# Attention steps inside a feed-forward stream: later mask products and row turns, a fourth rotating PSUM bank, one more step turned by TensorE

## The chip, the cores and the metric

The kernel runs on one core of one Trainium2 chip. The metric is the device time of one execution in microseconds (us), from the start to the end of the program on that core. Times are given as the median over several executions; a profile is one more execution, recorded by the hardware profiler, with its own time.

## What is computed

Eight batches of eight heads go through a windowed causal attention over 576 positions of 64 channels; the result is laid out as 4608 rows of 512 channels and goes through a multiplicative feed-forward network. Heads 0 to 3 look at the last 32 positions ("plain"), heads 4 to 7 at every fourth of the last 128 ("dilated").

```
scores = scale * np.matmul(q, k.transpose(0, 1, 3, 2))        # [8, 8, 576, 576]
mask_plain = (rel >= 0) & (rel < 32)
mask_dil = (rel >= 0) & (rel < 128) & (rel % 4 == 0)
attn = softmax(where(mask, scores, -1e9))
x = (attn @ v).transpose(0, 2, 1, 3).reshape(4608, 512)
a = x @ w1                    # 512 -> 1024
b = x @ w2
h = a * b @ w3                # 1024 -> 1024
out = h @ w_out               # 1024 -> 512
```

## The kernel before

**Tiling.** A batch's attention is cut into four *steps*, numbered 4b to 4b+3: the two halves of the positions for the dilated heads (u = 1; steps 4b and 4b+1), then the two halves for the plain heads (u = 0; steps 4b+2 and 4b+3). A step handles four heads and 288 positions. Its stations are:

- `scores`: 24 small matmuls into the four-bank PSUM tile `ps_a` (L313), one exponential over 128x1152 on ScalarE into the SBUF tile `et` (L343), and one product of `et` with the 0/1 mask on VectorE, in place (L344). In the kernel before, all three are emitted together.
- `values`: 12 matmuls with `et` as weights (L355) into another part of `ps_a`, then a reciprocal (L363) and a product (L366) on VectorE that leave the normalised rows in `xo`.
- `to_channels`: `xo` has to be turned so that channels lie on partitions, into `XT[u]`. Either six TensorE transposes into PSUM (L413) and a ScalarE copy (L419), or one transposing DMA on SyncE's queue (L404). The flag `by_dma` (L297) says which; before, it is true from step 8 on but for steps 10 and 11.

Queries and keys are loaded as rows (`qn`, `kn`) by GpSimd's DMA queue and turned on VectorE by stream transposes (L269, L277) into `qt` and `kt`; a batch needs 14 such *row turns*: four for each of dilated q, dilated k and plain q, and two longer ones for plain k. `qn` and `kn` have two buffers each, so the load for batch b+2 (L138) waits until the last row turn has read batch b's buffer. The stretch `prefetch(b)` emits the loads of q, k, the dilated v (`vd`) and the plain v (`vp`) in this order on GpSimd's queue.

**The feed-forward part.** w3 and w_out are first multiplied into one matrix `wf_sb` (`fuse_t`: transposes of w3 rows, L662 and L668; `fuse_m`: L676 and L684). Then, for each batch and half hf of the positions and each of eight blocks f, `ffn1` runs two *halves*, one with w1 and one with w2: four matmuls of 128x128 weights against 128x288 columns of `XT` each (L579), in the order dilated, dilated, plain, plain. The first half's sum is copied to SBUF by ScalarE (`asb`, L612), the second is multiplied with it on VectorE into `gt` (L619). `ffn2` takes a tile of 128 rows: eight matmuls over 512 columns (L646), a ScalarE copy (L653) and stores on SyncE's queue (L628).

**PSUM.** `bank()` hands out PSUM banks in rotation: three buffers called `f`. The eighth bank, `ps_x`, is used by `to_channels` and the first `fuse_t`; it joins the rotation as every fourth bank once batch 1 is done (L759 and L760). A half can only start when the reader of the bank's last contents (the copy L612 or L653, or the product L619) is done.

**Order of the work.** All is emitted in one order, written by the program, and each engine runs its instructions in that order. The feed-forward loops call `point(n)` before each half (0.57 units) and each half of an `ffn2` tile (1 unit). The attention is a list of *phases*, each with some `room`; `point` emits phases until the place in that list reaches what a straight line between `marks` asks for at this count of units. A mark says by which count a batch's steps must all be emitted: at the start of that batch's `ffn1`, less `ahead` units. `segment` builds the list for steps 8 to 31: in round i come `scores` of step i, an empty phase with two row turns, the turn of step i-2 where TensorE does it, `values` of step i-1 (with its transposing DMA, where DMA does it), and an empty phase with two more row turns. `second_batch` lists steps 4 to 7 with a fixed count of units for each. Batch 0 is emitted ahead of all this by `first_batch`.

Four banks of rotation and its order are decided in these lines:

```python
def bank():
    if "x" in late:
        late["x"] += 1
        if late["x"] % 4 == 0:
            return ps_x.bitcast(F32)
    return banks.tile([P, TB], F32, tag="f", name="f")
```

Of the kernel before, what the change touches and what calls it, by code (L numbers as in the profile page):

```python
# [12 lines left out]
BF16 = mybir.dt.bfloat16  # L13
# [3 lines left out]
ACT = mybir.ActivationFunctionType  # L17
# [6 lines left out]
HALF = 288  # L24
# [29 lines left out]
def kernel(  # L54
# [11 lines left out]
    nc = tc.nc  # L66
# [6 lines left out]
    KFF = d_ff // P  # L73
    NT = n_tok // TB
    scale = 1.0 / float(np.sqrt(D))
# [42 lines left out]
    ps_x = psum.tile([P, 2 * TB], BF16, name="ps_x")  # L118
    pool = four_banks()
    ps_s = [pool.tile([P, 2, TB], F32, name=f"ps_s{i}") for i in range(2)]  # L120
    late = {}
# [7 lines that stand above are left out]
# [163 lines left out]
    class Step:  # L292
        def __init__(self, n, b, u, hf):
            self.b, self.u, self.hf = b, u, hf
            self.et = ets[n % NET]

            self.by_dma = b > 2 or (b == 2 and u == 1)  # L297
            self.xo = {}

        def score_matmuls(self, heads, bank_of, start):  # L300
# [36 lines left out]
        def scores(self):  # L337

            ps_a = late["a"]
            self.score_matmuls(range(4), lambda h: ps_a[:, h], True)  # L340
            ev = self.probs(0, 4)
            mk = (mask_di if self.u else mask_pl[:, self.hf]).rearrange("p m x -> p (m x)")
            nc.scalar.activation(out=ev, in_=ps_a[:, :, 0:HALF], func=ACT.Exp, scale=scale)  # L343
            nc.vector.tensor_tensor(  # L344
                out=ev, in0=ev, in1=mk.unsqueeze(1).to_broadcast([P, 4, HALF]), op=AL.mult
            )
# [51 lines left out]
                        self.value_matmul(2 * hp + hl, m, ov[:, j // 3, j % 3, :])  # L398
            self.normalize(ov, self.xo.rearrange("p h j d -> p (h j) d"), 4, 3)()

        def to_channels(self, ps=ps_x, copy=nc.scalar.copy, hps=(0, 1)):
            dst = XT[self.u][:, 2 * self.b + self.hf]
            if self.by_dma:
                nc.sync.dma_start(  # L404
                    out=dst.rearrange("p h (m t) -> p (h m) t", m=3),
                    in_=self.xo[0:96].rearrange("p h (m e) d -> p (h m) (e d)", m=3),
                    transpose=True,
                )
                return
            xv = ps[:, 0 : 2 * HALF].rearrange("p (h x) -> p h x", h=2)  # L410
            for hp in hps:
                for m in range(3):
                    nc.tensor.transpose(  # L413
                        out=xv[:, hp, 96 * m : 96 * m + 96],
                        in_=self.xo[0:96, hp, 2 * m : 2 * m + 2, :],
                        identity=ident[0:96, 0:96],
                    )
            h = slice(hps[0], hps[-1] + 1)
            copy(out=dst[:, h], in_=xv[:, h])  # L419
# [3 lines left out]
    steps = [  # L423
        Step(4 * b + 2 * (1 - u) + hf, b, u, hf)
        for b in range(B)
        for u in (1, 0)
        for hf in range(2)
    ]
# [10 lines left out]
    def later(f, *args, after=1.0):  # L439

        phases.append([lambda: f(*args)])
        room.append(after)
# [5 lines left out]
    def first_batch():  # L448


        d0, d1, p0, p1 = steps[0:4]
        transpose_qk(0, 1, 0)
        transpose_qk(0, 1, 1)
        d0.scores_of_pair(0)
        d0.scores_of_pair(1)
        transpose_qk(0, 0, 0)
        d1.scores_of_pair(0)
        d1.scores_of_pair(1)
        transpose_qk(0, 0, 1)
        warm_up(4)  # L460
        p0.scores_of_pair(0)
        p0.scores_of_pair(1)
        warm_up(2)
        d0.values_of_pair(0)
        d0.values_of_pair(1)
        p1.scores_of_pair(0)
        warm_up(1)
        d1.values_of_pair(0)
        d1.values_of_pair(1)
        p1.scores_of_pair(1)  # L470
        d0.to_channels()
        p0.values_of_pair(0)
        p1.values_of_pair(0)
        pool = four_banks()
        ps_b = [pool.tile([P, TB], F32, name=f"ps_b{i}") for i in range(4)]
        late.update(b=ps_b, n=0)
        d1.to_channels(ps_b[0].bitcast(BF16))
        warm_up(1, ps_b[3])
        p0.values_of_pair(1)
        p0.to_channels(ps_x, hps=(0,))  # L480
        p1.values_of_pair(1)
        begin(0, 0, (2, 3))
        begin(0, 1, (2, 3))
        begin(0, 0, (0,))
        begin(0, 1, (0,))
        p0.to_channels(ps_x, hps=(1,))
        x1 = bank().bitcast(BF16)
        p1.to_channels(x1, nc.vector.tensor_copy, hps=(0,))
        begin(1, 0, (2, 3))
        begin(1, 1, (2, 3))  # L490
        begin(0, 0, (1,))
        begin(0, 1, (1,))
        p1.to_channels(x1, nc.vector.tensor_copy, hps=(1,))
        begin(1, 0, (0,))
        begin(1, 1, (0,))
        ffn1(0, 0, 0)
        begin(1, 0, (1,))
        begin(1, 1, (1,))
        const_masks()
        prefetch(2)  # L500
# [3 lines left out]
    def second_batch():  # L504

        d0, d1, p0, p1 = steps[4:8]
        for at, f, *args in (
            (19, transpose_qk, 1, 1, 0),
            (20, transpose_qk, 1, 1, 1),
            (22, d0.scores),  # L510
            (24, d1.scores),
            (26, d0.values),
            (26, transpose_qk, 1, 0, 0),
            (27, transpose_qk, 1, 0, 1),
            (28, d0.to_channels),
            (28, d1.values),
            (31, p0.scores),
            (32, d1.to_channels),
            (33, p1.scores),
            (35, p0.values),  # L520
            (37, p0.to_channels),
            (37, p1.values),
            (37, prefetch, 3),
            (37, transpose_qk, 2, 1, 0),
            (38, transpose_qk, 2, 1, 1),
            (39, p1.to_channels),
            (39, transpose_qk, 2, 0, 0),
        ):
            later(f, *args)
            when.append(at)  # L530

    def segment(lo, hi):


        pieces = []

        def some():
            for f in pieces[:2]:
                behind(f)
            del pieces[:2]  # L540

        for i in range(lo, hi + 1):
            at, b = i % 4, i // 4
            more = 4 * (b + 1) < hi
            if at == 0 and i < hi:
                pieces += transposes(b, 0, 1)
                for u, which in ((1, 0), (1, 1), (0, 0)) if more else ():
                    pieces += transposes(b + 1, u, which)
            if i < hi:
                later(steps[i].scores, after=0.8)  # L550
                later(lambda: None, after=0.8)
                some()
            if i > lo + 1 and not steps[i - 2].by_dma:
                later(steps[i - 2].to_channels, after=0.4)
                done_at[i - 2] = len(phases)
            if i > lo:
                later(steps[i - 1].values, after=0.8)
                if steps[i - 1].by_dma:
                    behind(steps[i - 1].to_channels)
                done_at[i - 1] = len(phases)  # L560
                if i < hi:
                    later(lambda: None, after=0.8)
                    some()
            if at == 2:
                behind(prefetch, b + 2)

# [89 lines left out]
    w3T = {}  # L656

    def fuse_t(ft):
        xv = bank().bitcast(BF16) if ft else ps_x
        xv = xv.rearrange("p (g x) -> p g x", g=KFF)  # L660
        for g in range(KFF):
            nc.tensor.transpose(  # L662
                out=xv[:, g, :],
                in_=w3n[ft // 2][:, ft % 2, g * P : (g + 1) * P],
                identity=ident,
            )
        w3T[ft] = wk_pool.tile([P, KFF, P], BF16, tag="w3T", bufs=3, name="w3T")
        nc.scalar.copy(out=w3T[ft], in_=xv)  # L668
# [44 lines left out]
    n0 = len(when)  # L713
    marks = [(40, n0)]
    for b in range(2, B):
        ahead = (0, 3, 6)[min(b - 2, 2)]
        marks.append((40 + 27.25 * (b - 1) - ahead, done_at[4 * b + 3]))
    place = np.concatenate([[0.0], np.cumsum(room)])
    xs, ys = [m[0] for m in marks], [place[m[1]] for m in marks]
# [1 line left out]
    def point(n):  # L721
        state[0] += n
        want = int(np.searchsorted(place, np.interp(state[0], xs, ys) - 1e-6))
        while state[1] < want and (state[1] >= n0 or state[0] >= when[state[1]]):
            for f in phases[state[1]]:
                f()
            state[1] += 1

    for f in range(1, KFF + 2):
        if f < KFF:  # L730
            ffn1(0, 0, f)
        if f == KFF:
            fuse_t(0)
        if f >= 2:
            ffn1(0, 1, f - 2)
# [14 lines left out]
    for b in range(1, B):  # L750
        for hf in range(2):
            for f in range(KFF):
                ffn1(b, hf, f, point)
                if due and f in (1, 3, 5):
                    ffn2(due.pop(0), point)
            while P * (done + 1) <= b * S + (hf + 1) * HALF:
                due.append(done)
                done += 1
        if b == 1:  # L759
            late["x"] = 0  # L760
    for t in due:
        ffn2(t, point)
    assert state[1] == len(phases)
# [30 lines left out]
```

## Time and profile before

| | us |
|---|---|
| median of 13 executions (lowest to highest) | 256.64 (255.66 to 257.82) |
| the profiled execution's own time | 257.65 |
| its span on the core, first to last instruction | 255.9 |
| TensorE (PE) matmuls busy in the span | 248.8 |
| VectorE (DVE) busy | 161.4 |
| ScalarE (ACT) busy | 119.4 |
| batch 1's feed-forward part begins, at TensorE | 64.1 |
| batch 2's begins (about) | 88.5 |

In the profile's rows a line such as L579 is the line of the kernel, followed by the engine, the operation, what it writes and reads, and how often. PE is TensorE's matmuls, PEld its weight loads, POOL is GpSimd, SP is SyncE. In a timeline row the first number is the start in us from the span's start, the second the duration; equal neighbours are merged, and "x8" says of how many instructions a row is made. Matmuls are pipelined, and the end of each is modelled, so the duration of one matmul (286 ns for 288 columns) is longer than the time from one start to the next. In a weight-load row, square brackets give the idle time ahead of it.

### The profile page before, as it was taken

The page shows a single profiled execution, that of the slowest core. Times are in us where ns is not written, and L with a number is a line of the kernel's source. Part 1 is how long each engine was busy: PE and PEld are TensorE (multiplying, and loading weights), DVE is VectorE, ACT ScalarE, POOL GpSimd, SP SyncE. Part 2 cuts the span into 40 slices and gives each one's busy share as a digit, 9 for nine tenths or more (in the row PEclk, how much of TensorE's full clock was granted, in tenths as well). Part 3 has the DMA queues.
Part 4 walks back from the last instruction along what each step waited for, and adds up shares of the span by engine and source line. Part 5 has one row for each costly group of instructions (what it writes and reads, how often), then busy time and mean ns, then how long its engine had stood idle before and what let it go on. Part 6 is the DMA issues. An engine that isn't in the chain of part 4 may idle for free.

```text
span 255.9 us, 6683 instructions
## 1 busy us (share of the span) xinstructions
PE 248.8 (97%) x2700; PEld 165.1 (65%) x2700; DVE 161.4 (63%) x379; ACT 119.4 (47%) x220; POOL 59.9 (23%) x87
## 2 busy tenths in 40 slices
PE   7899999999999999998999999999999999999995
PEld 2477764645665766665676766676767666777663
DVE  6676436867878766566685775577767543645550
ACT  2454356564644654544445444444444445333332
POOL 8984333737205201501061106000000000000000
DMA  6999999999999993999479957931313222312113
GB/s 102 166 188 200 206 212 200 190 201 204 252 191 153 170 214 89 144 180 160 92 105 163 186 102 111 158 88 35 96 26 94 57 64 67 105 29 79 40 44 123
DMA packets 66562, 33.81 MB, mean 132 GB/s; under 512 B 51556, under 2 KB 56932, under 8 KB 66532
## 3 DMA queue, kind: packets, MB, share of 16 engines
q0 software_dynamic: 47232, 20.70, 66.9%
q1 hardware_dynamic: 19300, 12.69, 21.9%
q8 instruction: 21, 0.34, 0.6%
q14 instruction: 9, 0.07, 0.1%
HBM read 41.39 MB, written 9.44 MB: 199 GB/s over the span
## 4 chain that ended last, share of the span: by engine, by line
PE 72%; DMA 19%; DVE 2%; POOL 2%; ACT 2%; issue 1%; POOLq 0%
PE f L579 30%; PE f L646 18%; PE ps_x L579 8%; DMA w3n<-in_moe_w_dram 6%; DMA XT<-xo 6%; PE ps_x L646 5%; DMA w_sb<-in_moe_w_dram 4%; PE ps_a L355 4%; PE f L676 3%; PE ps_a L313 3%; DMA kn<-in_k_dram 2%; POOL w_sb L177 2%; ACT et L343 2%; PE f L662 1%; PE ps_x L413 1%
## 5 line engine op out<-in xcount | busy, mean ns | idle before, releaser
L579 PEld LDWEIGHTS <-w_sb 128*128 128x128 bf16 x1024 | 97.2, 98 | 32.1 <-issue 3.3
L579 PE MATMUL f<-XT,w_sb 128*128 128x288 bf16 x704 | 100.8, 286 | 1.4 <-DMA XT<-xo 0.8
L619 DVE TENSOR_TENSOR gt<-f,asb 128x288 bf16<-128x288 f32 x91 | 45.2, 504 | 18.7 <-PE f L579 18.6
L646 PE MATMUL f<-wf_sb,gt 128*128 128x512 bf16 (+1 forms) x240 | 55.9, 372 | 0.0
L612 ACT CAST asb<-f 128x288 bf16<-128x288 f32 x85 | 34.0, 400 | 34.7 <-PE f L579 32.3
L646 PEld LDWEIGHTS <-gt 128*128 128x128 bf16 x296 | 27.7, 98 | 25.5
L343 ACT ACTIVATE et<-ps_a 128x1152 bf16<-128x1152 f32 x28 | 31.7, 1132 | 10.3 <-PE ps_a L313 10.3
L653 ACT COPY osb<-f 128x512 f32<-128x512 f32 (+1 forms) x30 | 17.1, 571 | 39.7 <-PE f L646 39.4
L166 POOL DMA_DIRECT2D vd<-in_v_dram x32 | 21.2, 670 | 54.3 <-PE ps_a L355 47.4
L579 PE MATMUL ps_x<-XT,w_sb 128*128 128x288 bf16 x192 | 31.4, 286 | 0.0
L366 DVE TENSOR_TENSOR xo<-ps_a,rcp 96x768 bf16<-96x768 f32 x28 | 26.7, 954 | 1.0
L344 DVE TENSOR_TENSOR et<-et,mask_pl 128x1152 bf16<-128x1152 bf16 x14 | 10.6, 759 | 19.2 <-ACT et L343 19.2
L277 DVE STREAM_TRANSPOSE qt<-qn 128x160 uint32<-128x160 uint32 (+1 forms) x64 | 21.2, 423 | 2.0 <-DMA qn<-in_q_dram 1.9
L344 DVE TENSOR_TENSOR et<-et,mask_di 128x1152 bf16<-128x1152 bf16 x14 | 10.6, 759 | 18.1 <-ACT et L343 18.1
L313 PEld LDWEIGHTS <-kt 32*128 32x128 bf16 x768 | 10.6, 92 | 11.9 <-issue 8.6
L355 PEld LDWEIGHTS <-et 128*128 128x128 bf16 x384 | 16.0, 98 | 3.4 <-ACT et L333 0.2
L579 PE MATMUL ps_b<-XT,w_sb 128*128 128x288 bf16 x128 | 16.5, 286 | 0.0
L612 ACT CAST asb<-ps_x 128x288 bf16<-128x288 f32 x27 | 10.8, 399 | 11.2 <-PE ps_x L579 11.2
L676 PE MATMUL f<-wo_sb,w3T 128*128 128x512 bf16 x64 | 16.0, 379 | 0.0
L646 PE MATMUL ps_x<-wf_sb,gt 128*128 128x512 bf16 x56 | 13.2, 379 | 0.0
L619 DVE TENSOR_TENSOR gt<-ps_x,asb 128x288 bf16<-128x288 f32 x21 | 10.2, 485 | 4.3 <-PE ps_x L579 4.3
L313 PE MATMUL ps_a<-qt,kt 32*128 32x96 bf16 x672 | 12.3, 202 | 0.2 <-DVE kt L277 0.2
(71 smaller groups left out, 178.1 us busy)
## 6 DMA issues: line engine op xcount, KB each, us to landing
out_dram<-osb SPq DMA_DIRECT2D x28, 144.0 KB
qn<-in_q_dram POOLq DMA_DIRECT2D x6, 576.0 KB, 10.0
kn<-in_k_dram POOLq DMA_DIRECT2D x6, 576.0 KB, 10.5
w_sb<-in_moe_w_dram POOLq DMA_DIRECT2D x8, 256.0 KB, 8.1
w3n<-in_moe_w_dram POOLq DMA_DIRECT2D x4, 512.0 KB, 14.2
vp<-in_v_dram POOLq DMA_DIRECT2D x5, 384.0 KB, 8.0
out_dram<-osb SPq DMA_DIRECT2D x10, 128.0 KB
qn<-in_q_dram POOLq DMA_DIRECT2D x4, 288.0 KB, 6.9
```

Of the source, the lines that this page charges most:

```text
L166: nc.gpsimd.dma_start(out=vds[b % 2][p0 : p0 + n, 4 * m : 4 * m + 4, 16 : 16 + 2 * D], in_=bass.AP(tensor=x.tensor, offset=x.offset + (4 * ...
L277: nc.vector.transpose(out=bass.AP(tensor=o.tensor, offset=o.offset + at, ap=[o.ap[0], [1, n], [9, 16], [step, 2]],), in_=t[:, k : k + 4 * ...
L313: nc.tensor.matmul(out=bank_of(h)[:, c0 : c0 + 96], lhsT=kt[prt, 96 * m : 96 * m + P, c], rhs=rhs, start=(start and c == 0), stop=(c == 1 ...
L343: nc.scalar.activation(out=ev, in_=ps_a[:, :, 0:HALF], func=ACT.Exp, scale=scale)
L344: nc.vector.tensor_tensor(out=ev, in0=ev, in1=mk.unsqueeze(1).to_broadcast([P, 4, HALF]), op=AL.mult)
L355: nc.tensor.matmul(out=out, lhsT=self.et[:, c0 : c0 + P], rhs=rhs, start=True, stop=True)
L366: nc.vector.tensor_tensor(out=xo[0:96].rearrange("p (n k) d -> p n k d", n=n), in0=ov[0:96, :, :, x0 : x0 + D], in1=rcp[0:96].unsqueeze(3) ...
L579: nc.tensor.matmul(out=ps[:, 0:HALF], lhsT=w_sb[:, c, f * P : (f + 1) * P], rhs=x, start=(c == 2), stop=(c == 1),)
L612: nc.scalar.copy(out=a_sb, in_=ps[:, 0:HALF])
L619: nc.vector.tensor_tensor(out=g, in0=pb, in1=a_sb, op=AL.mult)
L646: nc.tensor.matmul(out=y, lhsT=gt[:, f, g0 : g0 + P], rhs=wf_sb[:, f, c0 : c0 + n], start=(f == 0), stop=(f == KFF - 1),)
L676: nc.tensor.matmul(out=wf_ps[ft], lhsT=w3T[ft][:, g, :], rhs=wo_sb[:, g, :], start=(g == 0), stop=(g == KFF - 1),)
```

## The change

The mask product becomes a method of its own, `mask`, emitted one phase after the exponential, in the phase that was empty (and in `second_batch` by counts of its own). The row turns that prepare the next batch are spread differently over the four rounds of a batch: two behind the first round's scores, none behind its mask or values; then none and two; two and two; three and three. They stand behind the scores and no longer behind an empty phase after them. `ps_x` is in the rotation from the first `fuse_t` on, and `to_channels` and every `fuse_t` take their bank from the rotation. Step 9 (batch 2, dilated, second half) is turned by TensorE. The mark of batch 3 is set four units ahead, not three.

```diff
-            self.by_dma = b > 2 or (b == 2 and u == 1)
+            self.by_dma = b > 2 or (b, u, hf) == (2, 1, 0)
...
             ev = self.probs(0, 4)
+            nc.scalar.activation(out=ev, in_=ps_a[:, :, 0:HALF], func=ACT.Exp, scale=scale)
+
+        def mask(self):
+            ev = self.probs(0, 4)
             mk = (mask_di if self.u else mask_pl[:, self.hf]).rearrange("p m x -> p (m x)")
-            nc.scalar.activation(out=ev, in_=ps_a[:, :, 0:HALF], func=ACT.Exp, scale=scale)
             nc.vector.tensor_tensor(
...
-        def to_channels(self, ps=ps_x, copy=nc.scalar.copy, hps=(0, 1)):
+        def to_channels(self, ps=None, copy=nc.scalar.copy, hps=(0, 1)):
...
+            if ps is None:
+                ps = bank().bitcast(BF16)
...
             (22, d0.scores),
+            (23, d0.mask),
             (24, d1.scores),
+            (25, d1.mask),
...
             (32, d1.to_channels),
+            (32, p0.mask),
             (33, p1.scores),
+            (34, p1.mask),
...
-        def some():
-            for f in pieces[:2]:
+        def some(n):
+            for f in pieces[:n]:
                 behind(f)
-            del pieces[:2]
+            del pieces[:n]
...
+            n = ((2, 0), (0, 2), (2, 2), (3, 3))[at]
             if i < hi:
                 later(steps[i].scores, after=0.8)
-                later(lambda: None, after=0.8)
-                some()
+                some(n[0])
+                later(steps[i].mask, after=0.8)
...
                 if i < hi:
                     later(lambda: None, after=0.8)
-                    some()
+            if i < hi:
+                some(n[1])
...
     def fuse_t(ft):
-        xv = bank().bitcast(BF16) if ft else ps_x
-        xv = xv.rearrange("p (g x) -> p g x", g=KFF)
+        xv = bank().bitcast(BF16).rearrange("p (g x) -> p g x", g=KFF)
...
-        ahead = (0, 3, 6)[min(b - 2, 2)]
+        ahead = (0, 4, 6)[min(b - 2, 2)]
...
+    late["x"] = 0
     for f in range(1, KFF + 2):
...
-        if b == 1:
-            late["x"] = 0
```

More of the change, by code (lines that the diff above doesn't have):

```diff
@@ L470, in first_batch @@
         p1.scores_of_pair(1)
-        d0.to_channels()
+        d0.to_channels(ps_x)
         p0.values_of_pair(0)
```

## The prediction, made before the changed kernel was run

> **What bounds the kernel now.** I read the page's first part, then the waits, then the timeline of TensorE against its own pitch, then the chain.
>
> ```profile
> PE 248.8 (97%) x2700; PEld 165.1 (65%) x2700; DVE 161.4 (63%) x379; ACT 119.4 (47%) x220; POOL 59.9 (23%) x87
> ...
> L619 DVE TENSOR_TENSOR gt<-f,asb 128x288 bf16<-128x288 f32 x91 | 45.2, 504 | 18.7 <-PE f L579 18.6
> ...
> L343 ACT ACTIVATE et<-ps_a 128x1152 bf16<-128x1152 f32 x28 | 31.7, 1132 | 10.3 <-PE ps_a L313 10.3
> ...
> L344 DVE TENSOR_TENSOR et<-et,mask_pl 128x1152 bf16<-128x1152 bf16 x14 | 10.6, 759 | 19.2 <-ACT et L343 19.2
> ```
>
> TensorE is busy for 248.8 of 255.9 us, so at most 7.1 us of visible idle time can be won, part of it before the first operands arrive. The mask product (0.76 us) idles VectorE for 37.3 us in all (the waits: 27 times, 1.4 us each), because it stands in VectorE's queue right behind an exponential of 1.13 us. That is idle time of an engine at 63%; it costs only where TensorE waits for the `gt` products queued behind it.
>
> Whether it does can't be read from "busy", because ends of matmuls are modelled. The starts tell it. A row without a stall is the first below: 12 matmuls in 1.63 us, of which 0.16 is the last one's modelled tail, so 0.1225 us a matmul and 0.49 us a half of `ffn1`. The next rows are batch 1, with three banks:
>
> ```profile
> 129.27 1.63 PE L579 MATMUL f<-XT,w_sb 128*128 128x288 bf16 x12
> ```
> ```profile
> 64.10 2.34 PE L579 MATMUL f<-XT,w_sb 128*128 128x288 bf16 x16
> ...
> 72.69 3.12 PE L579 MATMUL f<-XT,w_sb 128*128 128x288 bf16 x20
> ...
> 73.98 0.76 DVE L344 TENSOR_TENSOR et<-et,mask_pl 128x1152 bf16<-128x1152 bf16 x1 [1.25 <-ACT et L343]
> 74.39 0.46 PEld L579 LDWEIGHTS <-w_sb 128*128 128x128 bf16 x4 [0.24 <-issue]
> 74.65 0.45 DVE L619 TENSOR_TENSOR gt<-f,asb 128x288 bf16<-128x288 f32 x1
> ...
> 75.16 0.34 PEld L579 LDWEIGHTS <-w_sb 128*128 128x128 bf16 x3 [0.31 <-issue]
> ```
>
> Twenty matmuls should take 20 x 0.1225 + 0.16 = 2.61 us; the row has 3.12, so 0.51 us was lost. TensorE's next weights come at 75.16, just after the product of 74.65 ended at 75.10 and freed its bank; that product stood behind the mask, the mask behind the exponential. The same subtraction over 64 to 91 us gives 0.22 (64.10), 0.39 (66.75: 8 matmuls end their pitch at 67.73, the next start is 68.12), 0.16 (68.12), 0.16 (70.11), 0.51 (72.69), 0.22 (83.72, a copy behind an exponential on ScalarE) and 0.11 (87.51): **1.77 us for want of a bank.** At 92.77 the turn of step 11 waits 0.23 us for `ps_x`, which a half has just used. From there on, with four banks and the same masks, no such row is left; two stalls remain, and the chain names them:
>
> ```profile
> 108.50 1.28 PE f L579 x11
> 109.78 8.18 DMA XT<-xo
> 118.00 0.90 PE f L579 x6
> ...
> 136.94 7.26 DMA XT<-xo
> 144.25 0.41 PE f L579 x2
> ```
>
> These are the transposing DMAs of steps 14 and 18, the plain first halves of batches 3 and 4. `ffn1` of the batch needs them at its third matmul. By the pitch TensorE was due at 117.03 and at 144.0, so the stalls are 0.97 and 0.27 us. Their packets are late because loads are in the same DMA engines: in the trace the transfer of step 24, with no load about, is through 2.1 us after its issue, that of step 14 7.7 us after. Recoverable in all: 1.77 + 0.23 + 0.97 + 0.27 = **3.24 us**.
>
> **The change, part by part.**
>
> *Fourth bank.* With three banks TensorE has two other halves, 0.98 us, before it needs a bank again; with four, 1.47 us, or 1.23 where a turn (six transposes, 0.26) takes a slot. The longest stall of the 1.77 is 0.39 us and the 0.51 is a 0.22 and a 0.29, all below the 0.49 gained. Turns and `fuse_t` now share the rotation. Their copies (L419 0.64, L668 1.01 us, ScalarE) end long before their bank returns: after `fuse_t` come a `fuse_m` of 1.73 us and more. I count that as nothing; it hides behind those matmuls, and without that cover a turn would hold its bank 0.64 - 0.40 = 0.24 us longer than a half.
>
> *Mask one phase later.* A phase is 1.7 units, some 1.46 us of TensorE work (an `ffn2` half is one unit and four matmuls of 0.217 us). The exponential ends about 0.4 + 0.1 + 1.13 = 1.65 us after the scores begin; the mask, emitted 1.46 us later and behind the `gt` products in between, finds it done. Nobody new waits: `values` of step i-1 come after the mask of step i, so each mask has a whole step (6.5 us and more) until its matmuls. In the second batch the shortest distance is the mask of step 7, at 34, to its values at 37: over 2.5 us of matmuls against 0.76. Cost nothing, if VectorE keeps up, which is the next point.
>
> *Row turns.* Their number stays. I worked the emission order out from the pacing arithmetic. Between the scores of step 8 and tile 4 of `ffn2`, batch 1's dense stretch, VectorE now has two long k turns (1.40), masks 8 to 10 (2.28), ten `gt` (5.04), four q turns (1.69) and two normalisations (2 x (0.22 + 0.95) = 2.34): 12.75 us. TensorE has 20 halves (9.8), three scores (0.37 + 0.22 of entry and exit each: 1.8) and two values (0.7): 12.3 us. Before, two more turns stood here (0.85) and some 4 us of waiting for exponentials. So VectorE falls behind by about 0.45 us plus what it brings along, against up to 1 us of bank slack. I keep **0.4 us** of the 3.24 as not won; the ends are 0 (slack holds) and 0.9 (half of the bank stalls stay). The turns also release loads on GpSimd's queue. Before, step 14's DMA (issue 109.78) had the load of `qn` for batch 6 beside it, issued at 108.38 just after the last q turn of batch 4. Now these three turns come behind two halves and their `gt` after values 14, so the load is issued about 0.35 + 0.86 + 0.98 + 0.45 + 1.3 = 3.9 us after these values begin, while the transposing DMA is issued 1.8 us after them (107.97 to 109.78). The same order arises for step 18. The k load that follows in the queue comes earlier than before, beside step 15's DMA, which has a half batch, over 10 us, of time. The `vd` and `vp` loads are tied to values, not to turns.
>
> *Batch 3's mark.* Values 14 and 18 now stand ahead of the second half of tiles 9 and 13: 4 x 0.217 = 0.86 us more TensorE work before their use, and on SyncE's queue their DMA goes ahead of that tile's stores, for which only `osb` with six buffers waits. With the load out of the way both stalls (1.24) should go; by the distance alone 0.97 - 0.86 = 0.1 would stay.
>
> *Step 9 by TensorE.* Removed: one DMA issue of 1.2 us on SyncE and its transfer, on which nothing waited (`ffn1` of batch 2 needs it at 88.5). Added: six transposes and a copy of 0.64 us on ScalarE (47% busy; hidden beside matmuls). The row of the same work:
>
> ```profile
> 86.39 0.42 PE L413 MATMUL ps_x<-ident,xo 96*128 96x96 bf16 x6
> 86.61 0.39 PEld L579 LDWEIGHTS <-w_sb 128*128 128x128 bf16 x4
> 86.65 0.40 ACT L612 CAST asb<-f 128x288 bf16<-128x288 f32 x1 [0.79 <-PE f L579]
> 86.65 0.53 PE L579 MATMUL f<-XT,w_sb 128*128 128x288 bf16 x3
> ```
>
> From the first transpose to the next matmul it is 86.65 - 86.39 = **+0.26 us** on TensorE. The Trainium skill speaks against this: "TensorE: Matmul & The Clock Gate", Part 4, gives about 275 ns for one transpose in a kernel, dominated by access latency. By it six cost 1.65 us, and my sum would be 1.4 us worse. The row decides: the transposes overlap, 42 ns apart.
>
> A second rule of the Trainium skill that speaks against the gain is in "DMA: Bandwidth & Descriptors", "Queues, rings and completion order": an engine takes its queues in turn and changes at packet boundaries. By it a transposing DMA beside loads would get a steady share, the order of the load would hardly matter, and only the 0.86 us of distance would count: 0.1 us less gained. Against that stand the 7.7 and 2.1 us. I go by the rows; it is little either way.
>
> **The sum.** -3.24 + 0.40 + 0.26 = -2.58 us on TensorE. It is made against the profiled execution: 257.65 us, span 255.9 and 1.75 around it, which gives 255.07. That execution lies 1.0 above the median of the runs shown; from 256.64 the forecast is **254.1 us**.
>
> **The rivals.**
> *The transfers stay late* (0.14): the transposing DMAs of steps 14 and 18 still lie behind `vp`, whose small packets filled the engines until 111 us, and nothing of the 1.24 is won: -2.58 + 1.24 = -1.34, 255.3. For: `vp` isn't moved. Against: the packets of `vp` end before those of `qn`.
> *Nothing measurable* (0.11): VectorE, not the bank count, sets batch 1's pace, as its 12.75 us against 12.3 allow, and all 1.77 stays; with late transfers too, 3.24 - 3.01 = 0.23 won, 0.26 spent, 256.7. Against: VectorE no longer idles at masks.
> *Slower* (0.10): three row turns (1.3 us) run straight into a mask (0.76) ahead of a `gt`: 2.06 us against the 1.47 of bank slack, 0.59 us at each of the ten places with three turns (two in each of batches 2 to 6), +5.9 - 2.58 = +3.3, 259.9. It decides from 0.33 us a place. Against: by the order, an `ffn2` half (0.86) or a `gt` mostly stands between them.
> The forecast has 0.65.
>
> **How the numbers follow.** A change of 0.3% (0.8 us) is about what the runs can tell from none. Faster: 0.65 + 0.14 = 0.79; same 0.11; slower 0.10. The forecast's own range runs from no loss at VectorE (-2.98, 253.7) to half of the bank stalls (-2.1, 254.5), widened by 0.4 for the median's spread: 253.3 to 254.9. The whole range reaches to the late transfers and their spread: 253.2 to 256.0, leaving out most of the last two cases.
>
> **What would show it.** Right: no row of `ffn1` matmuls between 64 and 90 us longer than its pitch by over 0.1; the mask rows without an exponential as releaser; 60 transposes at L413 become 66; no DMA of `XT` in the chain at batch 3. Wrong: PEld rows with issue gaps in 70 to 76 us (VectorE), gaps after three row turns, or the chain still led through a transposing DMA.

## The result

The changed kernel takes 254.57 us (median of 11 executions, 254.25 to 255.12), beside 256.99 us for the kernel before (median of 48, those shown ahead of the prediction among them). The ratio is 0.9907, with a 95% interval of 0.989 to 0.9924: faster by 0.9%, or 2.4 us. The forecast was 254.1 us, with a range of 253.2 to 256.0. The two profiled executions took 257.65 and 254.74 us, with spans of 255.9 and 253.0, so 2.9 us lie between them where my sum had 2.58. Between the medians it is 2.4: the profiled execution of before was itself 0.66 us slower than its median. An execution more than 1.5% above the fastest of its kernel is left out of the ratios, here and below, and "counted" means those that stay.

The chain's shares before:

```profile
PE 72%; DMA 19%; DVE 2%; POOL 2%; ACT 2%; issue 1%; POOLq 0%
```

The page of the changed kernel, its first part, its chain and the rows of the mask and of the `gt` products:

```profile
PE 247.5 (98%) x2706; PEld 165.6 (65%) x2706; DVE 163.4 (65%) x379; ACT 120.3 (48%) x221; POOL 59.9 (24%) x87
...
PE 82%; DMA 13%; POOL 2%; DVE 1%; issue 1%; ACT 0%; POOLq 0%
...
L631 DVE TENSOR_TENSOR gt<-f,asb 128x288 bf16<-128x288 f32 x78 | 38.7, 498 | 34.5 <-PE f L591 26.4
...
L347 DVE TENSOR_TENSOR et<-et,mask_pl 128x1152 bf16<-128x1152 bf16 x14 | 10.6, 754 | 4.0 <-ACT et L342 3.9
```

TensorE has six matmuls more (step 9's transposes) and 1.3 us less of busy time: the stalls of before were partly inside "busy". DMA has 13% of the chain instead of 19%, and what is left of it is the loads of the first 42 us; no transposing DMA stands in it. The waits of VectorE for an exponential at the mask fall from 37.3 to 4.5 us, six times instead of 27 (total in us, times, longest; before, then changed):

```profile
DVE et L344 <- ACT et L343: 37.3, 27, 2.9
```
```profile
DVE et L347 <- ACT et L342: 4.5, 6, 1.3
```

The time didn't leave VectorE: it now idles ahead of the `gt` products instead, for TensorE, as an engine with time to spare should.

TensorE's timeline in batch 1 (start, duration), the stretch whose rows were too long before by up to half a microsecond:

```profile
64.07 1.64 PE L591 MATMUL f<-XT,w_sb 128*128 128x288 bf16 x12
...
68.85 1.63 PE L591 MATMUL f<-XT,w_sb 128*128 128x288 bf16 x12
...
71.77 1.16 PE L591 MATMUL f<-XT,w_sb 128*128 128x288 bf16 x8
72.76 0.65 PE L591 MATMUL ps_x<-XT,w_sb 128*128 128x288 bf16 x4
73.25 0.65 PE L591 MATMUL f<-XT,w_sb 128*128 128x288 bf16 x4
```

12 x 0.1225 + 0.16 = 1.63: nothing is lost. Eight take 1.16 where 1.14 is due, and the next rows follow at the pitch. In all starts of matmuls after 43 us no gap of over 0.1 us above the pitch is left but at the entry and exit of the score matmuls, as before.

The queues of GpSimd and SyncE around step 14's transposing DMA, before:

```profile
108.38 0.70 POOL L138 DMA_DIRECT2D qn<-in_q_dram  x1 [2.98 <-DVE qt L277]
```
```profile
109.78 1.64 SPq L404 DMA_TRANSPOSE XT<-xo  x1
```

and changed:

```profile
102.25 1.43 POOL L159 DMA_DIRECT2D vp<-in_v_dram  x1
109.46 0.70 POOL L138 DMA_DIRECT2D qn<-in_q_dram  x1 [5.78 <-DVE gt L631]
```
```profile
107.20 1.20 SPq L407 DMA_TRANSPOSE XT<-xo  x1
108.49 4.34 SPq L640 DMA_DIRECT2D out_dram<-osb  x5
```

The transposing DMA is issued 2.3 us ahead of the load of `qn`, where before it came 1.4 us behind it, and ahead of the stores of tile 9. Its last packet is through 2.1 us after its issue instead of 7.7 (worked out from the trace's packets of that queue). The load of `vp` is still issued some 5 us ahead of it, so the rival that saw `vp` holding the transfer back is out. All fourteen profiled executions of this document say the same of steps 14 and 18: with the load of `qn` issued ahead of the transposing DMA (before, fourth bank alone, masks alone, even row turns, row turns in sixes) its last packet came 6.1 to 8.7 us after the issue, with the load behind it (the other nine) after 2.1 to 4.7.

### The profile page after: what moved, and what is told of

The parts are those of the page before. It is cut to its first block, busy times and chain, and to the rows that moved or that the text cites. A ratio compares the mean times of both kernels' runs of the same rounds, so it can differ in the third digit from the quotient of the medians.

```text
span 253.0 us, 6702 instructions
## 1 busy us (share of the span) xinstructions
PE 247.5 (98%) x2706; PEld 165.6 (65%) x2706; DVE 163.4 (65%) x379; ACT 120.3 (48%) x221; POOL 59.9 (24%) x87
## 4 chain that ended last, share of the span: by engine, by line
PE 82%; DMA 13%; POOL 2%; DVE 1%; issue 1%; ACT 0%; POOLq 0%
PE f L591 33%; PE f L658 18%; PE ps_x L591 11%; PE ps_x L658 7%; DMA w3n<-in_moe_w_dram 6%; PE ps_a L358 4%; PE ps_a L313 4%; DMA w_sb<-in_moe_w_dram 4%; PE f L687 3%; DMA kn<-in_k_dram 2%; POOL w_sb L177 1%; PE f L418 1%; PE ps_x L687 1%; PE ps_x L673 0%; PE f L673 0%
## 5 line engine op out<-in xcount | busy, mean ns | idle before, releaser
L591 PE MATMUL f<-XT,w_sb 128*128 128x288 bf16 x668 | 95.5, 286 | 0.0
L631 DVE TENSOR_TENSOR gt<-f,asb 128x288 bf16<-128x288 f32 x78 | 38.7, 498 | 34.5 <-PE f L591 26.4
L624 ACT CAST asb<-f 128x288 bf16<-128x288 f32 x89 | 35.6, 400 | 34.3 <-PE f L591 34.0
L658 PE MATMUL f<-wf_sb,gt 128*128 128x512 bf16 (+1 forms) x216 | 51.0, 375 | 0.0
L591 PE MATMUL ps_x<-XT,w_sb 128*128 128x288 bf16 x228 | 37.3, 286 | 0.0
L631 DVE TENSOR_TENSOR gt<-ps_x,asb 128x288 bf16<-128x288 f32 x34 | 17.5, 516 | 11.7 <-PE ps_x L591 11.6
L658 PE MATMUL ps_x<-wf_sb,gt 128*128 128x512 bf16 (+1 forms) x80 | 18.4, 368 | 0.0
L687 PE MATMUL f<-wo_sb,w3T 128*128 128x512 bf16 x56 | 14.1, 380 | 0.0
L366 DVE RECIPROCAL rcp<-ps_a 96x12 f32<-96x12 f32 x28 | 6.3, 223 | 11.3 <-PE ps_a L358 11.1
L624 ACT CAST asb<-ps_x 128x288 bf16<-128x288 f32 x23 | 9.2, 399 | 7.5 <-PE ps_x L591 7.3
L313 PE MATMUL ps_a<-qt,kt 32*128 32x96 bf16 x672 | 12.3, 202 | 0.0
## 6 DMA issues: line engine op xcount, KB each, us to landing
w_sb<-in_moe_w_dram POOLq DMA_DIRECT2D x8, 256.0 KB, 7.7
```

The lines of the kernel that those rows point to most:

```text
L313: nc.tensor.matmul(out=bank_of(h)[:, c0 : c0 + 96], lhsT=kt[prt, 96 * m : 96 * m + P, c], rhs=rhs, start=(start and c == 0), stop=(c == 1 ...
L591: nc.tensor.matmul(out=ps[:, 0:HALF], lhsT=w_sb[:, c, f * P : (f + 1) * P], rhs=x, start=(c == 2), stop=(c == 1),)
L624: nc.scalar.copy(out=a_sb, in_=ps[:, 0:HALF])
L631: nc.vector.tensor_tensor(out=g, in0=pb, in1=a_sb, op=AL.mult)
L658: nc.tensor.matmul(out=y, lhsT=gt[:, f, g0 : g0 + P], rhs=wf_sb[:, f, c0 : c0 + n], start=(f == 0), stop=(f == KFF - 1),)
L687: nc.tensor.matmul(out=wf_ps[ft], lhsT=w3T[ft][:, g, :], rhs=wo_sb[:, g, :], start=(g == 0), stop=(g == KFF - 1),)
```

## The experiments

The first 42 us of a run end with a wait for w3, and their end lies anywhere from 41.65 to 42.68 us in the profiled executions, whatever comes after; the changed kernel and its version with the mark at three, which do the same until then, differ by 0.67. For pieces of less than 1 us I therefore use a second measure beside the ratio: the time from batch 1's first feed-forward matmul to the end of ScalarE's last copy, read from the profiled execution ("the paced part"). It is 189.15 us before and 186.22 changed, 2.93 less. One kernel was profiled twice and gave 185.99 and 185.98. But it is one execution of each kernel, and not always a typical one: the last column sets the time of the profiled execution beside the median of that kernel's executions (the counted ones, for the kernels of this section). Where the two are far apart, the paced part shows where time goes in that execution, and the ratio what the change is worth. A ratio is taken over all counted executions and needn't be the quotient of two medians; 0.001 of it is 0.26 us.

| kernel | ratio to before (95% interval) | paced part, us | to before | profiled execution, us (median) |
|---|---|---|---|---|
| before | 1 | 189.15 | | 257.65 (256.99) |
| changed kernel | 0.9907 (0.989 to 0.9924) | 186.22 | -2.93 | 254.74 (254.57) |
| fourth bank alone | 0.9939 (0.992 to 0.9957) | 188.30 | -0.85 | 256.86 (255.43) |
| masks alone | 0.9985 (0.9965 to 1.0006) | 188.40 | -0.75 | 256.85 (256.19) |
| row turns alone | 1.0062 (1.0042 to 1.0082) | 189.98 | +0.83 | 258.81 (258.54) |
| changed, three banks | 0.9936 (0.9914 to 0.9959) | 186.87 | -2.28 | 254.89 (255.28) |
| changed, masks with exponentials | 0.9978 (0.996 to 0.9996) | 188.24 | -0.91 | 256.79 (256.70) |
| changed, even row turns | 0.9971 (0.995 to 0.9991) | 187.08 | -2.07 | 255.35 (256.39) |
| changed, mark at three | 0.9914 (0.9892 to 0.9936) | 186.22 | -2.93 | 254.06 (254.62) |
| changed, row turns in sixes | 0.9924 (0.9902 to 0.9946) | 186.53 | -2.62 | 255.29 (254.74) |
| changed, step 9 by DMA | 0.992 (0.9892 to 0.9948); again 0.9894 (0.9869 to 0.9919) | 185.99; 185.98 | -3.16 | 254.45 (254.70); 254.43 (254.41) |
| changed, steps 9 and 11 by DMA | 0.9939 (0.9908 to 0.997) | 189.52 | +0.37 | 257.83 (254.69) |
| changed, steps 4, 5, 7, 9, 11 by DMA | 1.0016 (0.999 to 1.0043) | 188.30 | -0.85 | 255.69 (257.49) |

### One part alone: the fourth bank

```diff
-        def to_channels(self, ps=ps_x, copy=nc.scalar.copy, hps=(0, 1)):
+        def to_channels(self, ps=None, copy=nc.scalar.copy, hps=(0, 1)):
...
+            if ps is None:
+                ps = bank().bitcast(BF16)
...
+    late["x"] = 0
     for f in range(1, KFF + 2):
...
```

> The kernel before with the fourth rotating bank alone (turns and fuse_t take their bank from it); masks, row turns, step 9 and the mark of batch 3 stay. My theory: the 1.77 us of bank stalls and the 0.23 us at ps_x go, the two waits for a transposing DMA (0.97 and 0.27 us) stay: 2.0 us faster than before, ratio 0.992. Rival (the mask behind its exponential is what holds the banks, and one bank more doesn't cover it): at least half of the 1.77 stays, 1.1 us faster at most, ratio 0.996 or more.

The bank stalls shrank as the theory said: three gaps of 0.1 us are left of 1.77. But only 0.85 us of the profiled paced part was won. TensorE's timeline and the chain of this kernel show where the rest went:

```profile
114.73 0.90 PE L581 MATMUL f<-XT,w_sb 128*128 128x288 bf16 x6
117.48 0.90 PE L581 MATMUL f<-XT,w_sb 128*128 128x288 bf16 x6 [1.85 <-DMA XT<-xo]
```
```profile
106.93 1.28 PE f L581 x11
108.22 9.22 DMA XT<-xo
117.43 0.04 issue
117.48 0.90 PE f L581 x6
```

TensorE came to batch 3 earlier and found the same transposing DMA still lying beside the loads; 114.73 + 6 x 0.1225 = 115.47 was due, 117.48 came: the wait had grown from 0.97 to 2.01 us. In this execution more than half of the bank's gain was given back at a wait that my sum had held fixed. It is the slowest of the 19 counted (256.86 us; the median is 255.43, the fastest 254.29). By the ratio the bank alone wins 1.6 us, so a typical execution seems to give back less; none of the quicker ones was profiled. Both the theory (0.992) and the rival (0.996 or more) missed the mechanism; the measured ratio lies between.

### One part alone: the masks

```diff
...
                 later(steps[i].scores, after=0.8)
-                later(lambda: None, after=0.8)
+                later(steps[i].mask, after=0.8)
                 some()
...
```

> The kernel before with the mask product emitted one phase after its exponential, nothing else. My theory: VectorE no longer idles behind exponentials (37 us fall to under 8), but with three banks a product of 0.76 us and the copies behind an exponential on ScalarE still hold banks: about 0.9 of the 1.77 us goes, both DMA waits stay: 0.9 us faster, ratio 0.9965. Rival (the mask is the cause of all): 1.6 us or more faster, ratio 0.994.

VectorE's waits for exponentials fell to 7.7 us as expected, and yet the bank stalls stayed: gaps of 0.21, 0.66, 0.16, 0.21 and 0.38 us add up to 1.62, where the theory had 0.9 left. The ratio, 0.9985, can't be told from 1. VectorE's and TensorE's timeline at the longest:

```profile
66.12 0.75 DVE L347 TENSOR_TENSOR et<-et,mask_di 128x1152 bf16<-128x1152 bf16 x1
...
66.78 1.25 DVE L269 STREAM_TRANSPOSE kt<-kn 128x288 uint32<-128x288 uint32 x2
...
67.88 0.87 DVE L626 TENSOR_TENSOR gt<-f,asb 128x288 bf16<-128x288 f32 x2
...
68.38 1.63 PE L586 MATMUL f<-XT,w_sb 128*128 128x288 bf16 x12 [0.50 <-DVE gt L626]
```

The mask no longer waits, but the two row turns still stand behind it, and both ahead of `gt`. The pair has moved together. Of the 0.75 us won, 0.32 lie in batch 1; the rest is at the transposing DMAs (0.79 us of waiting at batch 3 instead of 0.97, none at batch 4 instead of 0.27).

### One part alone: the row turns

```diff
...
+            n = ((2, 0), (0, 2), (2, 2), (3, 3))[at]
             if i < hi:
                 later(steps[i].scores, after=0.8)
+                some(n[0])
                 later(lambda: None, after=0.8)
-                some()
...
+            if i < hi:
+                some(n[1])
```

> The kernel before with the row turns spread as in the changed kernel, nothing else (masks behind their exponentials, three banks, step 9 by DMA, mark of batch 3 at three). Theory A, formed on the first four runs (the load of q that the turns release, not the distance, makes the DMA of step 14 late): that DMA is through in about 2 to 3 us, no wait for XT at batches 3 and 4 (-1.24 us), and of the 1.77 us of bank stalls some 0.7 go, since 0.85 us of row turns leave the stretch: span 254.0 us, 1.9 under before. Theory B (the distance of the mark is what counts): the wait of 0.97 us stays, span 255.2.

Slower than before, against both theories. Step 14's DMA was indeed through in 3.9 us and waited for only 0.23, and step 18's in 2.7, as theory A had it; but the bank stalls of batch 1 rose to 2.8 us, and a new one appeared in batch 4, where the rotation already has four banks:

```profile
159.88 0.76 DVE L344 TENSOR_TENSOR et<-et,mask_pl 128x1152 bf16<-128x1152 bf16 x1 [1.02 <-ACT et L343]
...
160.56 0.64 DVE L277 STREAM_TRANSPOSE kt<-kn 128x128 uint32<-128x128 uint32 x2
161.04 0.45 DVE L277 STREAM_TRANSPOSE qt<-qn 128x160 uint32<-128x160 uint32 x1
...
161.33 0.44 DVE L621 TENSOR_TENSOR gt<-ps_x,asb 128x288 bf16<-128x288 f32 x1
...
161.82 0.65 PE L581 MATMUL ps_x<-XT,w_sb 128*128 128x288 bf16 x4 [0.60 <-DVE gt L621]
```

1.02 us of waiting, a mask of 0.76 and three turns, all ahead of one `gt`: this is the slower rival of my prediction, with the wait for the exponential added to it. The turns behind the scores are good only if the mask isn't there yet, for then they run in the time that the exponential takes.

### One part undone: three banks; masks with their exponentials

The first takes the fourth bank out of the changed kernel until batch 1 is done; the turns and the first `fuse_t` go back to `ps_x`:

```diff
...
-    late["x"] = 0
     for f in range(1, KFF + 2):
...
+        if b == 1:
+            late["x"] = 0
```

> The changed kernel with three rotating banks until batch 1 is done, turns on ps_x as before. My theory: about 0.9 us of bank stalls comes back between 64 and 92 us, none at the transposing DMAs: 0.9 us slower than the changed kernel, ratio to before 0.994. Rival (masks alone do it): as fast as the changed kernel, 0.991.

Four gaps came back between 64 and 76 us (0.21, 0.11, 0.16, 0.16 us), none at a transposing DMA; the paced part is 0.65 us longer, and by the ratio the kernel loses 0.7. So with masks and turns in their new places, the bank is worth 0.65 and not the 1.77 that I had put to it; the rest of the change removes the other 1.1.

The second emits the product right behind the exponential again:

```diff
             nc.scalar.activation(out=ev, in_=ps_a[:, :, 0:HALF], func=ACT.Exp, scale=scale)
+            self.product()
 
         def mask(self):
+            pass
+
+        def product(self):
             ev = self.probs(0, 4)
```

> The changed kernel with the mask product back in one phase with its exponential, all else changed. Theory A, from the runs with one part alone (the row turns behind the scores are harmless only because they now fill the wait for the exponential; with the mask ahead of them they come on top of it): a gt stands behind 1.3 us of waiting, 0.76 of mask and up to 1.3 of turns, 3.4 us against 1.47 of slack; some 0.9 us of bank stalls in batch 1 and 0.8 in the later rounds with three turns: span 254.7, 1.7 over the changed kernel. Theory B (the parts simply add): the masks alone gave 0.75, span 253.8. Theory C (the fourth bank alone covers it): span 253.0.

Theory A was right in size: the span is 255.0, the paced part 2.02 us longer, and the ratio says 1.8. Three gaps make it up (0.22, 1.32 and 0.49 us). At the longest, in this kernel's timeline:

```profile
83.40 1.13 ACT L342 ACTIVATE et<-ps_a 128x1152 bf16<-128x1152 f32 x1
...
84.57 0.76 DVE L351 TENSOR_TENSOR et<-et,mask_di 128x1152 bf16<-128x1152 bf16 x1 [1.64 <-ACT et L342]
...
85.24 1.25 DVE L269 STREAM_TRANSPOSE kt<-kn 128x288 uint32<-128x288 uint32 x2
...
86.34 0.80 DVE L635 TENSOR_TENSOR gt<-f,asb 128x288 bf16<-128x288 f32 x2
...
86.83 0.65 PE L595 MATMUL f<-XT,w_sb 128*128 128x288 bf16 x4 [1.16 <-DVE gt L635]
```

Here a fourth bank is in rotation and isn't enough.

### The load, the distance, and the mark

```diff
-                some(n[0])
                 later(steps[i].mask, after=0.8)
+                some(2)
...
                 if i < hi:
                     later(lambda: None, after=0.8)
-            if i < hi:
-                some(n[1])
+                    some(2)
```

> The changed kernel with the even spread of row turns (two behind each mask and each values), all else changed. Theory A: the DMA of step 14 takes 7 to 9 us again; the mark at four gives 0.86 us of the wait back, so batch 3 waits 1.0 to 1.2 us for XT (the wait was 2.0 with the fourth bank alone), and 0.1 to 0.3 us of bank stalls return: span 254.3, 1.3 over the changed kernel. Theory B (distance): no wait for XT, span 253.1.

```diff
-        ahead = (0, 4, 6)[min(b - 2, 2)]
+        ahead = (0, 3, 6)[min(b - 2, 2)]
```

> The changed kernel with the mark of batch 3 at three units, as before. Theory A: the DMA of step 14 is issued ahead of the load and is through in 2 to 4 us, over 3 us before it is needed; no wait, span as the changed kernel's 253.0. Theory B (distance): a wait of 0.9 us for XT at batch 3, span 253.9.

With even turns the load of `qn` is back at its place (GpSimd's queue below), step 14's DMA takes 7.0 us, and still TensorE doesn't wait for it: it is issued at 108.09, its last packet is through at 115.10, and TensorE needs it at 115.88. Theory A missed there, in this execution and by less than the 0.86 us that the mark adds. The 0.86 us of the paced part that this kernel loses are two bank stalls of 0.39 and 0.46 us, ending at 68.1 and 86.7 us.

```profile
102.82 1.45 POOL L159 DMA_DIRECT2D vp<-in_v_dram  x1
107.34 0.70 POOL L138 DMA_DIRECT2D qn<-in_q_dram  x1 [3.08 <-DVE rcp L366]
```

That execution is the fastest of the 12 (255.35 us; the median is 256.39). By the ratio the even turns cost 1.6 us and not 0.86, so the others lose more than these two stalls. A wait for the transfer, as theory A had it, may be part of it; none of them was profiled, and this stays open.

With the mark at three, the load comes late as in the changed kernel, the DMA takes 3.3 us, and nothing waits either: the paced part is the same to 0.01 us. So the load's order is enough alone, and with it the mark's distance adds nothing; the mark may go back to three. That the distance would be enough without the order is shown for one execution only, with little to spare.

### The slower rival, driven up

```diff
-            n = ((2, 0), (0, 2), (2, 2), (3, 3))[at]
+            n = ((2, 0), (0, 0), (0, 6), (6, 0))[at]
```

> The changed kernel with the twelve row turns for the next batch run six at a time (behind the values of the third round and the scores of the fourth). This is the slower rival of the prediction driven up: 6 turns are 2.5 us on VectorE ahead of a gt, against 1.47 us of bank slack. By that rival's arithmetic 2.5 - 1.47 = 1.0 us at ten places less what stands between them: about 0.5 us each, span 258. If VectorE's idle time around them takes it up, as I argued, under 0.1 us each, span 253 to 254.

Six turns in a row cost two gaps of 0.18 and 0.12 us and 0.31 us of the paced part. The second gap stands at the third matmul of batch 3, the first that reads step 14's turn: here the load of `qn` was issued ahead of that DMA again, it took 7.5 us, and even with the mark at four TensorE seems to have waited for it (the profile names no releaser). The rival's 0.5 us at ten places didn't come: behind the scores the turns fill the exponential's time, and behind the values an `ffn2` tile often follows, 1.7 us without a `gt`. This reason is argued from the order of the work, not shown.

### Step 9, and more steps by DMA

```diff
-            self.by_dma = b > 2 or (b, u, hf) == (2, 1, 0)
+            self.by_dma = b > 2 or (b, u) == (2, 1)
```

> The changed kernel with step 9 turned by DMA, as before. My theory: its transfer lands before batch 2 needs it, so nothing waits, and TensorE is spared six transposes: 0.26 us faster than the changed kernel, ratio to before 0.9897. Rival (step 9's DMA would wait behind loads and hold batch 2's start): a wait for XT at about 86 us, and slower than the changed kernel.

> The changed kernel with step 9 turned by DMA once more, for the spread of its times: in the first run 3 of 11 executions took over 256 us, while 26 executions of three kernels with step 9 on TensorE and the same row turns (the changed one, its mark at three, turns in sixes) and of the one with three banks all took under 255.4. If the transfer is late in some executions, about a quarter of the new ones are over 255.5 us again and the rest lies at 254.0 to 255.0; if that was chance, none is, and the median is 254.3, 0.26 under the changed kernel's 254.57.

The paced part is shorter by 0.23 and 0.24 us, all of it in batch 1's stretch, where the six transposes stood (23.05 us to 22.78). Nothing waits for the transfer. The first run's times had a tail (two of the ten counted executions over 256 us, and the one left out), the second none (six from 253.92 to 254.74, median 254.41), so a late transfer is not shown, and not excluded; no execution of that tail was profiled. On these runs this is the fastest version by the trace; by the ratios the two cannot be told apart.

```diff
-            self.by_dma = b > 2 or (b, u, hf) == (2, 1, 0)
+            self.by_dma = b > 2 or (b == 2 and (u, hf) != (0, 0))
...
-        ahead = (0, 4, 6)[min(b - 2, 2)]
+        ahead = (6, 4, 6)[min(b - 2, 2)]
```

> The changed kernel with steps 9 and 11 turned by DMA (step 11 is needed half a batch later than step 10), and batch 2's mark six units ahead so that step 10's turn stays ahead of batch 2. My theory: two times 0.26 us spared on TensorE and no wait for XT, span 252.5, 0.5 under the changed kernel. Rival: step 11's DMA lies beside loads of q and k, takes over 13 us, and half of batch 2 waits: over 253.0.

```diff
-            self.by_dma = b > 2 or (b, u, hf) == (2, 1, 0)
+            self.by_dma = b > 2 or (b in (1, 2) and (u, hf) != (0, 0))
...
-        ahead = (0, 4, 6)[min(b - 2, 2)]
+        ahead = (6, 4, 6)[min(b - 2, 2)]
```

> As the last, and steps 4, 5 and 7 turned by DMA too. My theory: five times 0.26 us spared, span 251.7, if their transfers land: steps 4 and 5 have 16 and 12 us, step 7 about 12, in a stretch where loads fill the DMA engines. Rival: step 5's or 7's DMA is late, as step 8's takes over 10 us here, and batch 1 waits for XT by 1 us or more: over 252.7.

In the profiled executions both fail by the rival's way. With steps 9 and 11, two waits of 1.3 us for `XT` appear (at 86 and 104 us), and a third gap of 1.3 us amid the value matmuls at 98 us for which the profile names no releaser; that one stays open. The wait at 104 us is for step 11: by the chain its DMA is issued at 85.83 us and releases TensorE 19.65 us later. But this execution is the slowest of the 11 counted. Six of them took 254.26 to 254.69 us, as the changed kernel does, and five 256.41 to 257.83: the transfers are late in some executions and not in others, and the paced part in the table is one of the late ones. With five steps all 13 counted executions are slower than the changed kernel's slowest. In the profiled one, the fastest, step 7's DMA takes 10.8 us and batch 1's second half waits for it, as this kernel's chain and TensorE's timeline say (a second wait for `XT`, of 0.76 us, stands at batch 2's start):

```profile
63.14 10.84 DMA XT<-xo
```
```profile
71.44 0.90 PE L591 MATMUL f<-XT,w_sb 128*128 128x288 bf16 x6
74.02 0.40 PE L591 MATMUL f<-XT,w_sb 128*128 128x288 bf16 x2 [1.67 <-DMA XT<-xo]
```

In these stretches the DMA engines are busy for 90% or more of the time (the pages show it for every slice from 7 to 100 us), and a turn of 0.26 us on TensorE is the cheaper one.

## Why the prediction was right, and where it wasn't

**What is recoverable: right.** I listed 3.24 us of gaps by subtracting the pitch from TensorE's rows; the changed kernel has none of them left, and its paced part is 2.93 shorter after paying for step 9. Of the signs that I named, one came only in the main: six of the 28 masks still wait for their exponential.

**The 0.4 us kept back for VectorE: too much.** From 12.75 us of work on VectorE against 12.3 on TensorE I charged the 0.45 as lost, although the banks had up to 1 us of slack for it; the gaps are zero. This term is the difference between the 2.58 of the forecast and the 2.93 measured, on the profiled executions.

**The step from the profile to the median: not sound, and it helped by luck.** I took the gaps of an execution of 257.65 us off a median of 256.64, as if the median execution had them all. With the 48 executions now known, the profiled one lies 0.66 us above the median; the medians differ by 2.42 us, less than my 2.58. So a part of the listed gaps is likely absent from a typical execution of before, and the 0.4 us held back for VectorE stood in for it. Only one execution of before was profiled, so this is an estimate and not shown. The spread points the same way: the changed kernel's executions lie within 0.9 us, those of before ahead of the prediction within 2.2.

**Fourth bank: right that it fits, wrong in what it is worth.** That each stall is shorter than the 0.49 us gained held but for the three gaps of 0.1 us left with the bank alone. But I put all 1.77 us to the bank. Undoing it costs 0.65. And alone it wins 0.85 of the profiled paced part (1.6 us by the ratio), since there 1.0 us goes to the longer wait at batch 3. A gap that is listed with a length has that length only as long as what comes before it stays; when TensorE gets faster ahead of a transfer, the wait for the transfer grows.

**Mask: "cost nothing" right, but no gain was given to it.** I counted the mask's move as neither gain nor cost and left the gain to the bank. Undoing it costs 2.02 us (1.8 by the ratio), the most of all parts, though alone it wins only 0.75 (0.4 by the ratio, which can't be told from none). It earns by making room: the row turns run in the exponential's time.

**Row turns: the load right, the sign of the rest by luck.** That the load of `qn` falls behind step 14's DMA, and that the DMA is then quick, came as worked out, and holds over all the runs. That they are harmless on VectorE holds only with the masks moved; alone they make the kernel slower (1.0062). My slower rival named this mechanism (turns and mask ahead of a `gt`) but not its condition, a mask still waiting in front of the turns.

**Mark: its 0.86 us of distance is not needed once the load comes behind the DMA.** The paced part is the same without it.

**Step 9: +0.26 us predicted, 0.23 and 0.24 measured by its undoing.** The price per transpose that the Trainium skill gives ("TensorE: Matmul & The Clock Gate", Part 4), some 275 ns, would by my estimate have made it 1.65. One transpose lasts 206 ns in the trace, not far from that; but six start 42 ns apart, and a sum of durations isn't the time that they take. The other rule weighed, on queues taking turns at packet boundaries ("DMA: Bandwidth & Descriptors", "Queues, rings and completion order"), left too little to the load's order as I applied it: 2.1 us against 7.0 with only the turns and so the load moved, in runs with the same mark.

The three parts alone sum to -0.85 - 0.75 + 0.83 = -0.77 us; with step 9's cost that is -0.5, and together they give -2.93. By the ratios it is -0.4 without step 9's cost, against -2.4. The forecast got the total because it was made from the gaps, not from the parts.

## What to carry to other kernels

List the gaps of the engine that sets the time, against its own pitch, and ask which of them a change leaves; that sum can hold even where the shares of the parts are wrong. When an engine works in order, judge what stands ahead of the instruction that others wait for as one sum: a wait, a product and a transposition in a row are one delay, and moving one of them may only move the pair. And where a wait ends with a transfer, time won ahead of it is not won until the transfer comes earlier too. Last, a profile is one execution: set its time beside the median before its gaps are given a price.

## What the runs showed of the hardware

A transposing DMA of one step takes 2.1 us from its issue to its last packet with no load about (step 24 before). With the load of `qn` issued ahead of it, at steps 14 and 18, it takes 6.1 to 8.7 us with the same 576 packets; before, at step 14, its first packet came 4.3 us after its issue. Issued ahead of that load it takes 2.1 to 4.7. In a stretch full of loads one took, by the chain, 19.7 us to the end of the wait for it (step 11, with steps 9 and 11 by DMA). Six 96x96 transposes on TensorE, 206 ns each in the trace, start 42 ns apart and take 0.25 us in a stream of matmuls.
